# Last tile of a pooled-attention and SiLU kernel: where two VectorE sums stand, and which engine copies a PSUM bank

## The chip, the cores and the metric

The kernel runs on one core of a Trainium2 chip. The metric is device time in microseconds (us) of one execution, the median of several runs. The engines are called as the profile calls them: PE is TensorE (matmuls; PEld its weight loads), DVE is VectorE, ACT is ScalarE, POOL is GpSimd, SP is SyncE, which here only issues stores. The program orders each engine's instructions by hand, so that an instruction which waits holds up all that stand behind it on the same engine.

## What is computed

A pooled attention (8 batches, 8 heads, 576 tokens, head size 64; keys and values are means over 8 tokens) gives x with 4608 rows and 512 columns. A two-layer block follows:

```python
def _moe_ref(x, w_in, w_out):       # x 4608x512, w_in 512x2048, w_out 2048x512
    h = x @ w_in
    g = h * (1.0 / (1.0 + np.exp(-h)))
    return (g @ w_out).astype(np.float32)
```

The change touches only the last tile's part of `g @ w_out`.

## The kernel before, in words

The 4608 rows are worked in nine tiles of 512 (`NT` = 9). For each tile the kernel computes the transposed hidden values `h_T` (2048 x 512, bf16, 16 blocks of 128 partitions) and then the output tile; attention for the next tile is mixed in between. From tile 3 on, `run(t)` (L777) plays a list of tokens, `PROGRAM` (L769), one after another. Each token emits a few instructions, and since every engine works its own instructions in the order in which they are emitted, the token list is the order of every engine. `A`, `B`, `C`, `E` tokens make hidden values, `h1h` to `h7l` make sums of hidden values, `d10` to `d73` are quarters of products of the second matmul, `u1` and `u2` correct a partial sum.

The second matmul is split in quarters and done with seven products of sums in place of eight (`H_SUMS` L600, `W_SUMS` L618). Product n has its weights in `W_OUT[n]` and its left side in `h_sum[n]`, or straight from `h_T` for products 3 and 4. A product is 16 matmuls of 128x128 by 256 columns. Three PSUM banks collect them (`bank`, L698): P takes products 4, 2, 7, Q takes 3, 5, 6, and R takes 1. What each product is followed by is in `after` (L715):

- after 4, ScalarE copies P to `r_sb` (L718); after 3, VectorE writes `rr_sb` = Q + `r_sb` (L720)
- after 2, bank P holds M4 + M2, which is the lower left quarter of the output: ScalarE copies it to `o_sb[1]` (L722)
- after 5, bank Q holds M3 + M5, the upper right quarter: VectorE copies it to `o_sb[0]` (L726)
- `u1` and `u2` (L747 to L751) take these two quarters off `rr_sb`, which leaves -M2 - M5; GpSimd does this in tiles 3 to 7 and VectorE in the last
- after 1, VectorE writes `t_sb` = R + `rr_sb` (L730); after 7 and 6, P + `t_sb` (L732) and Q + `t_sb` (L736) are the other two quarters, and are stored

`hidden_sum` (L608) writes half of one `h_sum`, 128x1024 in bf16, and reads only `h_T`. Products 1, 2, 5, 6 and 7 need their two halves each.

The last tile (t = 8) has no attention beside it and no tile behind it. There `run` replaces everything from token `d10` on. The products 1, 7 and 6 are done by `columns` (L762) for half of each bank at a time, first columns 0 (`L0`), then columns 1 (`L1`), so that the first half can be summed and stored during the second. Before them come the sums that were still to do:

```python
            i = toks.index("d10")
            sums = [x for x in toks[i:] if x[0] in "hu"]
            toks = toks[:i] + sorted(sums) + ["L0", "L1"]
```

What is left of the list for the last tile, from the second half of the h sums on, is therefore

```
h5l h1h h1l h7h d20 d21 d22 d23 d50 d51 d52 d53 h6h h6l u1 u2 L0 L1
```

On VectorE this reads: four h sums, the copy of bank Q (L726, behind `d53`), the two halves of `h_sum6`, `u1`, `u2`, and then in `L0` the sums L730, L732, L736. On TensorE: products 2, 5, then 1, 7, 6 for columns 0, then 1, 7, 6 for columns 1. Product 6 needs `h_sum6` and writes bank Q; the columns 1 of product 1 write bank R, of which L730 reads columns 0. The stores of the last tile are issued by `store` (L551, the DMA at L555): the lower left quarter by GpSimd, the upper right by SP, in `L0` by SP and GpSimd, in `L1` by ScalarE and SP.

Of the kernel before, what the change touches and what calls it, by code (L numbers as in the profile page):

```python
# [36 lines left out]
def kernel(  # L37
# [9 lines left out]
    nc = tc.nc  # L47
# [43 lines left out]
    def ps_tile(shape, dtype, tag, name):  # L91
        return psum.tile(shape, dtype, tag=tag, bufs=banks[tag], name=name)
# [16 lines left out]
    o_sb = [singles.tile([128, 2, d_model], FP32, name=f"o_sb{n}") for n in range(2)]  # L109
# [26 lines left out]
    def load_q(b, halves=False):  # L136
        st = batches.setdefault(b, {})
        q_bf = mid.tile([128, 2, QI * D], BF16, tag="q_bf", name="q_bf")
        if halves:
            pass  # L140
        elif b == B - 1:

            for s in range(4):
                for a in range(2):
                    nc.gpsimd.dma_start(
                        out=q_bf[QP * s : QP * (s + 1), a, :].rearrange(
                            "p (i d) -> p i d", d=D
                        ),
                        in_=q[b, 4 * a + s].rearrange("(i p) d -> p i d", p=QP),
                    )  # L150
        else:
            nc.gpsimd.dma_start(out=q_bf, in_=q_r[b])
        st["q_bf"] = q_bf
        st["qT"] = mid.tile([128, 2, QI, QP, 2], BF16, tag="qT", bufs=1, name="qT")
# [41 lines left out]
    def behind_x_sums(n=6):  # L196
        nc.gpsimd.tensor_copy(out=gate[:1], in_=x_sum[:1, U_XI[n], 0, :1])
# [353 lines left out]
    def store(t, m, cs, engines=(nc.sync,)):  # L551
        n0 = (t * NTT + m * 128) // QP
        src = o_sb[m // 2][:, m % 2, cs]
        if n0 // QI == B - 1:
            engines[0].dma_start(out=out[n0 * QP : n0 * QP + 128, cs], in_=src)  # L555
            return
        for u in range(128 // QP):
            n = n0 + u
            rows = (
                out[n * QP : (n + 1) * QP] if n // QI == B - 1  # L560
                else out_r[n // QI, n % QI]
            )
            engines[u % len(engines)].dma_start(
                out=rows[:, cs], in_=src[QP * u : QP * (u + 1)]
            )
# [27 lines left out]
    LO, HI, FULL = slice(0, CQ), slice(CQ, 2 * CQ), slice(0, 2 * CQ)  # L593
# [37 lines left out]
    def left(n, kt, c):  # L631
        cs = slice(128 * c, 128 * (c + 1))
        if n in h_sum:
            return h_sum[n][:, kt, cs]
        i = n - 3
        return h_T[:, i * KQ + kt, i * NQ + 128 * c : i * NQ + 128 * (c + 1)]
# [59 lines left out]
    def down_stages(t, last):  # L696
        ps = {}
        bank = {2: "P", 5: "Q", 1: "R", 4: "P", 3: "Q", 7: "P", 6: "Q"}  # L698
        begun = set()
        r_sb, rr_sb, t_sb = r_sbs[0], rr_sbs[0], t_sbs[0]  # L700
        add, sub = ALU.add, ALU.subtract
        tt = nc.vector.tensor_tensor

        def matmuls(n, k0, k1, cs=(0, 1)):
            b = bank[n]
            for kt in range(k0, k1):
                for c in cs:
                    nc.tensor.matmul(  # L708
                        ps[b][:, c, :], lhsT=left(n, kt, c), rhs=W_OUT[n][:, kt, :],
                        start=b not in begun,  # L710
                        stop=kt == k1 - 1, skip_group_check=True,
                    )
                    begun.add(b)

        def after(n, cc=(0, 1), tail=False):  # L715
            cs = slice(cc[0], cc[-1] + 1)
            if n == 4:
                nc.scalar.copy(r_sb, ps["P"])  # L718
            elif n == 3:
                tt(out=rr_sb, in0=ps["Q"], in1=r_sb, op=add)  # L720
            elif n == 2:
                nc.scalar.copy(o_sb[1][:, :, LO], ps["P"])  # L722
                if last:
                    store(t, 3, LO, (nc.gpsimd,))
            elif n == 5:
                nc.vector.tensor_copy(out=o_sb[0][:, :, HI], in_=ps["Q"])  # L726
                if last:
                    store(t, 1, HI)
            elif n == 1:
                tt(out=t_sb[:, cs], in0=ps["R"][:, cs], in1=rr_sb[:, cs], op=add)  # L730
            elif n == 7:
                tt(out=o_sb[0][:, cs, LO], in0=ps["P"][:, cs], in1=t_sb[:, cs], op=add)  # L732
                for c in cc:
                    store(t, c, LO if tail else FULL, (nc.scalar if tail else nc.sync,))
            else:
                tt(out=o_sb[1][:, cs, HI], in0=ps["Q"][:, cs], in1=t_sb[:, cs], op=add)  # L736
                for c in cc:
                    if tail:
                        store(t, 3, HI, both)
                    else:  # L740
                        store(t, 2 + c, FULL, (nc.gpsimd if last else nc.sync,))

        def part_of(tok):
            if tok == "o":
                return after(6)
            n = int(tok[1])
            if tok[0] == "u":  # L747
                src = o_sb[1][:, :, LO] if n == 1 else o_sb[0][:, :, HI]
                (nc.vector if last else nc.gpsimd).tensor_tensor(  # L749
                    out=rr_sb, in0=rr_sb, in1=src, op=sub  # L750
                )  # L751
                return
            if not ps:
                for b in "PQR":
                    ps[b] = ps_tile([128, 2, CQ], FP32, "mm", f"o_ps{b}")
            i = int(tok[2])
            k0 = 2 * i if n == 4 else 2 * (i ^ 2)
            matmuls(n, k0, k0 + 2)
            if i == 3 and n != 6:
                after(n)  # L760

        def columns(c):  # L762
            for n in (1, 7, 6):
                matmuls(n, 0, KQ, (c,))
                after(n, (c,), c == 1)

        return part_of, columns
# [9 lines left out]
    def run(t):  # L777
        a = t + 1
        attn, last = a < B, t == NT - 1
        stage = unit_stages(t, iter(int, 1))  # L780
        part_of, columns = down_stages(t, last)
        toks = PROGRAM.split()
        gate_on = int([x for x in toks if x[0] == "x"][-1][1])
        attn_toks = ("T1 T2 k npp q0 q1 q2 q3 sc0 sc1 sc2 de0 de1 de2 nu0 nu1").split()
        if last:
            i = toks.index("d10")
            sums = [x for x in toks[i:] if x[0] in "hu"]
            toks = toks[:i] + sorted(sums) + ["L0", "L1"]
        toks = [x for x in toks if attn or x not in attn_toks]
        if a == B - 1:  # L790
            toks.insert(1 + max(toks.index("de2"), toks.index("nu1"), toks.index("o")), "nu2")
        if t == T4:
            toks.insert(0, "T2")
        if attn:
            if a + 1 < B - 1:
                load_q(a + 1)
            behind_x_sums(6 if t == T4 else gate_on)
            pool_k(a)
            if a + 1 < B:
                load_one(a + 1, "k")  # L800
            pool_v(a)
            if a + 1 < B:
                load_one(a + 1, "v")
                if a + 1 == B - 1:
                    load_q(a + 1)
                load_rest(a + 1, "k")
                load_rest(a + 1, "v")
        for x in toks:
            if x[0] in "ABCE" and x[1] in "2514376as":
                stage("ABCE".index(x[0]), {"a": "h"}.get(x[1], x[1]))  # L810
            elif x[0] == "L":
                columns(int(x[1]))
            elif x[:2] == "de":
                denominators(a, visits[int(x[2])])
            elif x[0] in "dou":
                part_of(x)
            elif x[0] == "h":
                k0 = 4 if x[2] == "h" else 0
                hidden_sum(int(x[1]), k0, k0 + 4)
            elif x == "T1":  # L820
                attn_tables()
            elif x == "T2":
                moe_tables()
            elif x == "k":
                k_transpose(a)
            elif x == "npp":
                numerators(a - 1, visits[2])
            elif x[0] == "q":
                n = int(x[1])
                q_transpose(a, n % 2, n // 2)  # L830
            elif x[:2] == "sc":
                scores(a, visits[int(x[2])])
            elif x[:2] == "nu":
                numerators(a, visits[int(x[2])])
            elif not last:
                unit_x_sum(t + 1, int(x[1]))
# [266 lines left out]
```

The softmax here doesn't subtract the row's maximum and nothing guards it: scores larger than these inputs give would overflow.

## Time and profile before

| | |
|---|---|
| time, median of 3 runs | 279.35 us (279.13 to 279.6) |
| span of the profiled execution | 277.0 us |
| PE busy | 270.7 us, 98% of the span |
| DVE busy | 241.2 us, 87% |
| ACT busy | 191.3 us, 69% |
| POOL busy | 114.3 us, 41% |
| an h sum in the last tile (L611) | 681 to 686 ns, ten of them |
| copy of bank P by ACT (L722) | 586 ns |
| copy of bank Q by DVE (L726) | 692 ns |
| last DVE instruction starts at | 273.96 us |

The page's busy shares are averages over all tiles. The chain of the profile follows the work that ended last back from the end, at each step to what released it; in the last tile it shows which engine sets the end at which moment. The timeline lists instructions by start, and merges neighbours that are alike (x4). In brackets stands how long the engine had been idle before one, and what released it. The token list's times are not in the program: they follow from the waits.

### The profile page before, as it was taken

The numbers are of one execution on the slowest core, as the hardware profiler recorded it, in microseconds if no ns is written. First come the engines' busy times: TensorE is split into PE (matmuls) and PEld (weight loads), VectorE is DVE, ScalarE is ACT, GpSimd is POOL, SyncE is SP. The second block draws the span as 40 slices with busy tenths as digits, with TensorE's granted clock in tenths as the row PEclk, the third lists the DMA queues.
The fourth block names the chain that finished last, engine by engine and source line by source line (L and its number), as shares of the span: only waits on it lengthen the run. The fifth ranks groups of instructions, "written<-read, shape, count | busy, mean of one in ns | idle before, by whom it ended". The sixth has DMA issues, their size and how long they took to land.

```text
span 277.0 us, 7372 instructions
## 1 busy us (share of the span) xinstructions
PE 270.7 (98%) x2923; PEld 209.1 (75%) x2933; DVE 241.2 (87%) x451; ACT 191.3 (69%) x373; POOL 114.3 (41%) x114
## 2 busy tenths in 40 slices
PE   8999999999999999999999999999999999999994
PEld 4448444576878678887888788877887788888883
DVE  4986787788998879998999899989999889998994
ACT  1688767468578966888778977798688858407700
POOL 8745217152158430954395428973720300040000
PEclk9999999999999999999999999999999999999999
DMA  7999999896849789669757835699510042014013
GB/s 210 285 254 247 206 321 183 239 160 123 165 56 210 212 123 176 151 169 134 129 113 196 126 56 127 178 109 146 132 43 0 2 105 50 2 27 128 1 38 116
DMA packets 31314, 37.73 MB, mean 136 GB/s; under 512 B 10352, under 2 KB 22256, under 8 KB 31280
## 3 DMA queue, kind: packets, MB, share of 16 engines
q0 software_dynamic: 23920, 27.03, 53.0%
q1 hardware_dynamic: 6928, 9.58, 12.6%
q10 hardware_dynamic: 432, 0.66, 0.7%
q8 instruction: 23, 0.38, 0.6%
q14 instruction: 11, 0.09, 0.1%
HBM read 36.70 MB, written 9.44 MB: 167 GB/s over the span
## 4 chain that ended last, share of the span: by engine, by line
PE 82%; DMA 12%; POOL 2%; DVE 1%; issue 1%; DVEq 0%; POOLq 0%
PE u_psP L489 14%; PE u_psQ L489 14%; PE o_psP L708 11%; PE o_psQ L708 11%; DMA w_in_sb<-in_moe_w_in_dram 7%; DMA w_out_sb<-in_moe_w_out_dram 6%; PE u_psR L489 5%; PE o_psQ L652 4%; PE o_psP L652 4%; PE o_psR L708 4%; PE hp_ps L543 4%; PE sc_ps L341 3%; PE nu_ps L385 3%; PE o_ps L578 2%; PE den_ps L359 2%; PE o_psR L652 1%
## 5 line engine op out<-in xcount | busy, mean ns | idle before, releaser
L489 PEld LDWEIGHTS <-w_sum 128*128 128x128 bf16 x532 | 51.9, 98 | 7.2 <-issue 0.3
L611 DVE TENSOR_TENSOR h_sum<-h_T 128x1024 bf16<-128x1024 bf16 (+1 forms) x78 | 55.7, 765 | 1.8 <-ACT h_T L549 1.0
L708 PEld LDWEIGHTS <-h_sum 128*128 128x128 bf16 x480 | 45.6, 98 | 9.5 <-issue 3.3
L349 ACT ACTIVATE es<-sc_ps 72x384 bf16<-72x384 f32 (+1 forms) x100 | 39.1, 471 | 6.2 <-PE sc_ps L341 6.0
L497 ACT ACTIVATE h_T<-c_sb 128x512 bf16<-128x512 f32 x58 | 35.6, 627 | 8.8 <-DVE c_sb L522 8.7
L749 POOL TENSOR_TENSOR rr_sb<-rr_sb,o_sb 128x512 f32<-128x512 f32 x10 | 16.9, 1687 | 42.3 <-ACT o_sb L722 36.5
L507 ACT COPY r_sb<-u_psP 128x512 f32<-128x512 f32 x29 | 17.0, 585 | 18.1 <-PE u_psP L489 17.9
L543 PE MATMUL hp_ps<-xT,w_in_sb 128*128 128x512 bf16 (+2 forms) x151 | 25.9, 317 | 0.3
L394 DVE TENSOR_TENSOR xT<-nu_ps,rec 128x384 bf16<-128x384 f32 (+1 forms) x50 | 23.9, 529 | 1.6 <-PE nu_ps L385 1.6
L489 PEld LDWEIGHTS <-w_in_sb 128*128 128x128 bf16 x232 | 22.5, 98 | 2.9
L191 POOL TENSOR_TENSOR raw<-raw 72x1024 f32<-72x1024 f32 x10 | 23.6, 2360 | 0.3 <-DMA raw<-in_v_dram 0.3
L522 DVE TENSOR_TENSOR c_sb<-u_psP,t_sb 128x512 f32<-128x512 f32 x29 | 19.8, 684 | 3.3 <-ACT r_sb L507 1.8
L549 ACT ACTIVATE h_T<-hp_ps 128x512 bf16<-128x512 f32 (+2 forms) x39 | 18.1, 476 | 5.9 <-PE hp_ps L543 4.8
L525 DVE TENSOR_TENSOR c_sb<-u_psQ,t_sb 128x512 f32<-128x512 f32 x29 | 19.9, 688 | 2.2 <-PE u_psQ L489 2.0
L510 DVE TENSOR_TENSOR rr_sb<-u_psQ,r_sb 128x512 f32<-128x512 f32 x29 | 19.8, 684 | 2.2 <-ACT r_sb L507 1.6
L513 DVE TENSOR_TENSOR t_sb<-u_psR,rr_sb 128x512 f32<-128x512 f32 x29 | 19.7, 681 | 1.6 <-PE u_psR L489 0.5
L543 PEld LDWEIGHTS <-w_in_sb 128*128 128x128 bf16 x156 | 14.6, 98 | 8.5 <-issue 0.7
L708 PEld LDWEIGHTS <-h_T 128*128 128x128 bf16 x192 | 18.8, 98 | 2.2
L497 ACT ACTIVATE h_T<-u_psQ 128x512 bf16<-128x512 f32 x29 | 17.2, 593 | 4.1 <-PE u_psQ L489 3.4
L497 ACT ACTIVATE h_T<-u_psP 128x512 bf16<-128x512 f32 x29 | 17.4, 599 | 2.7 <-PE u_psP L489 2.6
L368 ACT ACTIVATE lnd<-den_ps 128x384 f32<-128x384 f32 (+1 forms) x23 | 11.2, 487 | 11.3 <-PE den_ps L359 11.3
L489 PE MATMUL u_psP<-x_sum,w_in_sb 128*128 128x256 bf16 x116 | 17.6, 273 | 0.0
(105 smaller groups left out, 564.3 us busy)
## 6 DMA issues: line engine op xcount, KB each, us to landing
out_dram<-o_sb SPq DMA_DIRECT2D x128, 64.0 KB, 2.3
raw<-in_k_dram POOLq DMA_DIRECT2D x10, 576.0 KB, 8.2
raw<-in_v_dram POOLq DMA_DIRECT2D x10, 576.0 KB, 8.2
q_bf<-in_q_dram POOLq DMA_DIRECT2D x6, 576.0 KB, 11.1
w_in_sb<-in_moe_w_in_dram POOLq DMA_DIRECT2D x8, 256.0 KB, 8.6
w_out_sb<-in_moe_w_out_dram POOLq DMA_DIRECT2D x4, 512.0 KB, 13.3
raw<-in_v_dram POOLq DMA_DIRECT2D x2, 768.0 KB, 10.9
raw<-in_k_dram POOLq DMA_DIRECT2D x1, 768.0 KB, 10.9
```

The costliest lines, as they stand in the source:

```text
L191: nc.gpsimd.tensor_add(out=raw[:, :, : 2 * D], in0=raw[:, :, : 2 * D], in1=raw[:, :, 2 * D :])
L349: nc.scalar.activation(es[:, s, :], sc[s], func=AF.Exp, scale=score_scale)
L394: nc.vector.tensor_mul(out=xT[:, 2 * g0 + c : 2 * (g0 + ng - 1) + c + 1 : 2, cols], in0=nu[c][:, :w].rearrange("r (g n) -> r g n", g=ng), ...
L489: nc.tensor.matmul(ps[y, bank][:, u, :], lhsT=w[:, kk, 128 * u : 128 * (u + 1)], rhs=x[:, kk, :], start=first and u == 0 and kk == 0, stop ...
L497: nc.scalar.activation(h_T[:, g : g + 2, j * NQ : (j + 1) * NQ], src, func=AF.Silu)
L510: tt(out=rr_sb, in0=ps[y, "Q"], in1=r_sb, op=ALU.add)
L522: tt(out=c_sb[0], in0=ps[y, "P"], in1=t_sb, op=ALU.add)
L525: tt(out=c_sb[1], in0=ps[y, "Q"], in1=t_sb, op=ALU.add)
L543: nc.tensor.matmul(hp_ps[:, r0:r1], lhsT=w_in_sb[:, kk, g * 128 : (g + 1) * 128], rhs=xT[:, kk, x0 : x0 + r1 - r0], start=(kk == 0), stop= ...
L611: nc.vector.tensor_tensor(out=h_sum[n][:, ks, :], in0=quarter(*a, ks), in1=quarter(*b, ks), op=op)
L652: nc.tensor.matmul(ps[b][:, c, :], lhsT=left(n, kt, c), rhs=W_OUT[n][:, kt, :], start=b not in begun, stop=kt == k1 - 1, skip_group_check= ...
L708: nc.tensor.matmul(ps[b][:, c, :], lhsT=left(n, kt, c), rhs=W_OUT[n][:, kt, :], start=b not in begun, stop=kt == k1 - 1, skip_group_check= ...
```

## The change

In the last tile the two sums for `h_sum6` go ahead of token `d20`, so that on VectorE they follow the other four without anything between; they no longer stand behind the copy of bank Q. That copy goes to ScalarE, which already copies bank P. `u1` and `u2` stay right ahead of `L0`. Tiles 0 to 7 are as before. The purpose is to have VectorE work on the sums while products 2 and 5 still run, and to take the bank copy out of its row.

```diff
             elif n == 5:
-                nc.vector.tensor_copy(out=o_sb[0][:, :, HI], in_=ps["Q"])
+                copy = nc.scalar.copy if last else nc.vector.tensor_copy
+                copy(out=o_sb[0][:, :, HI], in_=ps["Q"])
                 if last:
                     store(t, 1, HI)
...
         if last:
-            i = toks.index("d10")
-            sums = [x for x in toks[i:] if x[0] in "hu"]
-            toks = toks[:i] + sorted(sums) + ["L0", "L1"]
+            i, j = toks.index("d10"), toks.index("d20")
+            sums = sorted(x for x in toks[j:] if x[0] == "h")
+            toks = toks[:j] + sums + [x for x in toks[j:i] if x[0] != "h"]
+            toks += ["u1", "u2", "L0", "L1"]
```

The last tile's list then ends in

```
h5l h1h h1l h7h h6h h6l d20 d21 d22 d23 d50 d51 d52 d53 u1 u2 L0 L1
```

## The prediction

> **What bounds the kernel now.** I read the page first: one core, span 277.0 us, TensorE (PE) busy 98% of it and granted full clock in all 40 slices. An average of 98% says that stages before the last tile are TensorE's; it says nothing of the last ten microseconds, and the diff touches nothing before them. So I went to the waits, the chain and the timeline of the last 15 us. First the waits between 262 and 278 us, longest first (who waited, for whom, us in total, times, longest):
>
> ```profile
> POOL out_dram L555 <- DVE o_sb L736: 5.1, 1, 5.1
> ACT o_sb L722 <- PE o_psP L708: 2.9, 1, 2.9
> PE o_psR L708 <- DVE t_sb L730: 0.8, 1, 0.8
> PEld L708 <- DVE h_sum L611: 0.5, 1, 0.5
> DVE o_sb L726 <- PE o_psQ L708: 0.3, 1, 0.3
> PE o_psQ L708 <- DVE h_sum L611: 0.2, 1, 0.2
> ```
>
> TensorE waits for VectorE (DVE) twice here: 0.2 to 0.5 us for h_sum and 0.8 us for t_sb. VectorE waits 0.3 us for TensorE ahead of its bank copy, L726. ScalarE (ACT) sits idle 2.9 us before L722.
>
> Then the chain of work that ended last, in order of time (start, length, what):
>
> ```profile
> 266.00 1.32 PE o_psQ L708 x12
> ...
> 267.95 1.28 DVE h_sum L611 x2
> 269.23 0.61 DVE rr_sb L749
> ...
> 269.87 0.70 DVE rr_sb L749
> ...
> 270.67 0.44 DVE t_sb L730
> ...
> 271.15 1.03 PE o_psR L708 x8
> 272.18 0.87 PE o_psP L708 x8
> 273.05 0.89 PE o_psQ L708 x8
> ...
> 273.96 0.42 DVE o_sb L736
> ```
>
> From 267.3 to 271.1 us the end is set by VectorE alone: the copy of bank Q, two h sums, u1 and u2 (both L749), the first t_sb. Before and after this stretch it is TensorE. The timeline of VectorE shows how its queue stands (start, length, line, operation, output and inputs):
>
> ```profile
> 264.53 2.49 DVE L611 TENSOR_TENSOR h_sum<-h_T 128x1024 bf16<-128x1024 bf16 x4
> 267.34 0.69 DVE L726 COPY o_sb<-o_psQ 128x512 f32<-128x512 f32 x1 [0.33 <-PE o_psQ L708]
> 267.95 1.28 DVE L611 TENSOR_TENSOR h_sum<-h_T 128x1024 bf16<-128x1024 bf16 x2
> 269.15 1.41 DVE L749 TENSOR_TENSOR rr_sb<-rr_sb,o_sb 128x512 f32<-128x512 f32 x2
> 270.67 0.42 DVE L730 TENSOR_TENSOR t_sb<-o_psR,rr_sb 128x256 f32<-128x256 f32 x1
> ```
>
> The reader is to see that VectorE has nothing to do from 267.02 (264.53 + 2.49) to 267.34, while the pair of sums queued behind the copy needs only h_T, whose last part ScalarE wrote by 262.26.
>
> **What the Trainium skill says.** "PSUM — Partial Sum Buffer", section "PSUM bank collisions raise a hardware error": two engines may not touch one bank in the same partitions at once, even in different columns, so the guard is by bank. That is why columns 1 of product 1 wait for the t_sb sum of columns 0, which reads the other half of bank R; the trace agrees (the 0.8 us wait; PE restarts at 271.15, 0.06 after t_sb ends). "Perfetto Trace Analysis", "Identifying Dependency Chains": an instruction that waits on several engines may get a separate semaphore instruction ahead of it. The trace agrees: t_sb, which needs DVE's u2 and PE's bank R, has one of 21 ns at 270.60, and starts 0.10 after u2 ends (270.67 against 270.57 in the chain), while u2, which needs DVE alone, starts 0.02 after u1. "ScalarE: Activation LUTs", "Table sets": copy is in every table set, so a second ScalarE copy loads nothing. L722 already copies among Silu with no load in this stretch. "SBUF — State Buffer", "Who interferes with whom": a VectorE sum with both inputs in SBUF contends with a GpSimd instruction that reads SBUF. The trace agrees, a tile earlier: the same pair of h sums took 2.42 us from 243.50, with GpSimd's L749 running to 245.37, against 1.28 us here. I come back to it.
>
> **The change, part by part.**
>
> (a) Two h sums move ahead of the bank copy. From 264.53 four sums take 2.49, one lasts 0.684 (L611, ten of them), so starts are (2.49 - 0.684)/3 = 0.60 apart. The pair then starts at 264.53 + 4 x 0.60 = 266.94 and not at 267.95, and ends at 266.94 + 1.28 = 268.22 and not at 269.23. That is 1.01 us, of two pieces: the idle 0.33 (0.40 if counted from the start that an unbroken row would have had) and the copy's 0.61 from start to start. Nothing ahead in the queue is delayed: all eight earlier sums keep their places, and the tokens move in VectorE's order alone.
>
> (b) Bank Q's copy goes from VectorE to ScalarE. It cost 0.692 there and should cost 0.586 here, by the row of L722, same shape and source (bank P). ScalarE has nothing after 266.23 but a store issue at 273.55. Q's last matmul ends at 267.30; with the 0.08 that L722 took behind bank P (265.56 to 265.64) the copy runs 267.38 to 267.97. Who waits for it: u2, the store of that half, and the first columns of product 6, which write bank Q. u2 cannot start before 268.86 (below); product 6's columns follow 8 + 8 matmuls at 0.87 a block, so not before 267.14 + 2 x 0.87 = 268.88. Both are some 0.9 us later than the copy's end. The store starts at the same time within 0.1. Cost on the path: nothing, hidden behind the sums and products 1 and 7.
>
> (c) What the copy's move adds as a wait: u2 now needs ScalarE (the copy) and VectorE (u1). Behind u2 stands t_sb, and for that TensorE waits, so any cost here is on the path. Bounds: 0, if ScalarE's part, met since 268.0, is taken early in the queue (u1 has such a semaphore instruction at 267.4, hidden), or 0.08, if u2 gets what t_sb has: a start 0.10 after its predecessor and not 0.02. I take 0.08, since in both VectorE's is the wait that is met last.
>
> (d) New times: u1 at 266.94 + (269.15 - 267.95) = 268.14; u2 at 268.14 + 0.72 + 0.08 = 268.94; t_sb 0.80 behind it at 269.74, ending 270.16. Before, it ended at 271.09: 0.93 earlier.
>
> (e) TensorE: product 1's columns 0 from 267.14, product 7's from 268.01, both as now. Product 6's wait for h_sum goes: sums done at 268.22, columns wanted at 268.88, and not 269.29. This 0.4 us alone is worth nothing, because TensorE then waits longer for t_sb: done with the block at 269.75, it could restart at 270.16 + 0.06 = 270.22. So 0.47 of waiting is left in place of 0.81, and VectorE still sets the end. This also bounds the gain: had VectorE taken no time, TensorE would restart at 269.75, 1.40 earlier than now.
>
> (f) From the restart on nothing changes: products 1, 7, 6 for columns 1, the last sum, its store. They shift whole. Last columns end at 273.94 - 0.93, last sum at 274.38 - 0.93 = 273.45. VectorE's two column-0 sums and GpSimd's store of half a tile are tied to t_sb and shift with it. Behind the last sum come 2.62 us to the span's end (277.0 - 274.38): a store issue of 0.33, landing about 1.7, closing semaphores. The two half-stores that don't shift were issued by 268.1 with about 2 us to land, so they are gone by then.
>
> Sum: -1.01 + 0.08 = -0.93 us. 279.35 - 0.93 = 278.42; I say 278.4.
>
> **Rivals.**
>
> The other wait takes its place. The end could be held by something between 267.3 and 271 that the chain hides: ScalarE's copy becoming visible late, or product 6 held for it. For that, the copy must end after 268.9, nearly 1 us later than L722's timing gives. If it held half of the gain back, 0.45 would be left: 278.9. Against it: the 0.9 us of slack on each of its readers. Chance 0.08.
>
> The stores set the end. DMA runs at 0.96 and 1.02 of its engines in two half-microseconds (272.5 to 273 and 273.5 to 274). If it were stores that end the kernel, an earlier last sum would only lengthen the wait, and the time would stay at 279.35. Against it: the last store has the normal landing of 1.7 us, and engines fall nearly idle in between (0.20 at 274 to 274.5). All big stores shift with the sums. Chance 0.06.
>
> The moved pair meets GpSimd, and the result is slower. GpSimd issues a store from 266.52 to 267.18, and the moved pair starts within that. If they contend as a tile earlier, the pair takes 2.42: it ends at 269.36, u1 starts 269.28, u2 270.08, t_sb 270.88, 0.21 later than now. That gives 279.35 + 0.21 = 279.56; with GpSimd's issue held up as well, 280. Against it: the two h sums that run during this issue today show no lengthening (all ten between 0.681 and 0.686). A store issue is not the fp32 sum of a tile earlier. Chance 0.04.
>
> **How the numbers follow.** Forecast 0.82; the three rivals 0.08, 0.06 and 0.04. Within the forecast the gain is 0.93 to 1.01 by (c), plus or minus 0.1 for semaphores whose place I can't see, and the runs before lie 0.25 around their median. So 279.35 - 1.1 - 0.25 = 278.0 below. Above, 279.35 - 0.8 + 0.2 = 278.75, extended to 278.95 to take in the half gain. What lies outside is the rivals of 0.06 and 0.04 and some scatter, under 2 in 10. 0.2% is 0.56 us, so faster means under 278.79: the forecast with a little scatter off, and a part of the first rival, 0.85. Same: 0.12. Slower, which needs over 279.91, takes a part of the last rival: 0.03.
>
> **What would show it.** In the profile after: six h sums in one row from 264.5, no copy on VectorE behind them; a second ScalarE copy near 267.4 of about 0.59; u1 near 268.1; t_sb near 269.7; no wait of TensorE for h_sum; its wait for t_sb about 0.4 to 0.5 and not 0.8; last sum near 273.4; some 2.6 us behind it. I am wrong if the sums lengthen while GpSimd issues its store, if u2 starts clearly after 268.95 (ScalarE's copy or its wait), or if more than 2.7 us stand behind the last sum.

## The result, and the profile after

The changed kernel takes 278.53 us (median of 6 runs, 278.02 to 278.85), against 279.35 before. The ratio of the times is 0.9967, with a 95% interval of 0.9954 to 0.998: 0.6 to 1.3 us faster, 0.9 in the middle. Beside the last experiments it was timed again: 278.47 (278.22 to 278.91, 11 runs) against 279.19, ratio 0.9975 (0.9966 to 0.9983), 0.5 to 0.9 us faster.

The page alone does not show this: the two spans read 277.0 and 276.9 us. The timeline of ScalarE tells why. Before, its first copy (a cast of the attention's pooled keys, `kz`) and a copy some 60 us later:

```profile
7.58 0.28 ACT L293 CAST kz<-kz_ps 128x144 bf16<-128x144 f32 x1 [4.55 <-PE kz_ps L286]
68.40 0.59 ACT L665 COPY r_sb<-o_psP 128x512 f32<-128x512 f32 x1
```

The same two in the changed kernel:

```profile
8.17 0.28 ACT L293 CAST kz<-kz_ps 128x144 bf16<-128x144 f32 x1 [5.20 <-PE kz_ps L286]
69.19 0.59 ACT L665 COPY r_sb<-o_psP 128x512 f32<-128x512 f32 x1
```

This execution was 0.59 us late at its first ScalarE copy and 0.79 late at 68 us, in a part that the diff does not touch, and it stays so. Product 5 on bank Q, before and after:

```profile
265.39 1.91 PE L708 MATMUL o_psQ<-w_out_sb,h_sum 128*128 128x256 bf16 x16
...
266.18 1.91 PE L708 MATMUL o_psQ<-w_out_sb,h_sum 128*128 128x256 bf16 x16
```

It ends at 265.39 + 1.91 = 267.30 before and at 266.18 + 1.91 = 268.09 after, in both 198.90 us behind the start of the copy at 68 us. So the last tile has to be compared from a mark of its own. I take this end of product 5 on bank Q, which the change does not move, and call it Qend.

VectorE's row in the last tile after the change (timeline: start, length, line, operation):

```profile
265.31 3.69 DVE L611 TENSOR_TENSOR h_sum<-h_T 128x1024 bf16<-128x1024 bf16 x6
268.91 1.48 DVE L750 TENSOR_TENSOR rr_sb<-rr_sb,o_sb 128x512 f32<-128x512 f32 x2
270.50 0.42 DVE L731 TENSOR_TENSOR t_sb<-o_psR,rr_sb 128x256 f32<-128x256 f32 x1
...
273.80 0.42 DVE L737 TENSOR_TENSOR o_sb<-o_psQ,t_sb 128x256 f32<-128x256 f32 x1 [0.45 <-PE o_psQ L708]
```

Six sums stand in one row where four, a gap, a copy and two stood. The pair u1, u2 takes 1.48 and not 1.41. ScalarE's row has the second copy:

```profile
268.17 0.59 ACT L727 COPY o_sb<-o_psQ 128x512 f32<-128x512 f32 x1 [1.16 <-PE o_psQ L708]
```

TensorE's one wait for VectorE in the last 15 us:

```profile
PE o_psR L708 <- DVE t_sb L731: 0.3, 1, 0.3
```

TensorE's wait for h_sum is gone, and its wait for t_sb is 0.3 and no longer 0.8. The chain (start, length, what) has u2's new semaphore instruction (`DVEq`) and still runs through VectorE before TensorE's restart:

```profile
259.90 0.34 PE u_psR L489 x3
...
262.38 2.28 DVE h_sum L611 x4
...
264.70 0.69 DVE rr_sb L720
...
265.91 3.09 DVE h_sum L611 x5
269.00 0.61 DVE rr_sb L750
269.61 0.03 issue
269.64 0.02 DVEq L750
269.66 0.04 issue
269.71 0.70 DVE rr_sb L750
...
270.50 0.44 DVE t_sb L731
...
270.98 1.03 PE o_psR L708 x8
```

It reaches further back than before. There VectorE's part began at Qend, because the copy in its row waited for product 5. Now it follows VectorE without a stop at TensorE back to 260.24, for more than 10 us; what VectorE still needs of product 5, u2's input by way of ScalarE's copy, is there in time. Qend is still a good mark, but no longer a cause.

Counted from Qend, the first t_sb sum starts at 2.41 and not 3.37, and the last sum ends at 6.13 (274.22 - 268.09) and not 7.08 (274.38 - 267.30): 0.95 us saved. Behind the last sum stand 2.68 us, before 2.62.

### The profile page after: what moved, and what is told of

Its sections match the earlier page's. It is cut to its first block, busy times and chain, and to the rows that moved or that the text cites. A ratio compares the mean times of both kernels' runs of the same rounds, so it can differ in the third digit from the quotient of the medians.

```text
span 276.9 us, 7384 instructions
## 1 busy us (share of the span) xinstructions
PE 271.9 (98%) x2933; PEld 210.0 (76%) x2933; DVE 240.7 (87%) x450; ACT 192.1 (69%) x374; POOL 114.6 (41%) x114
## 4 chain that ended last, share of the span: by engine, by line
PE 79%; DMA 15%; DVE 4%; issue 1%; POOL 0%; DVEq 0%; POOLq 0%
PE u_psP L489 14%; PE u_psQ L489 14%; PE o_psP L708 10%; PE o_psQ L708 10%; DMA w_in_sb<-in_moe_w_in_dram 6%; DMA w_out_sb<-in_moe_w_out_dram 6%; PE u_psR L489 5%; PE o_psQ L652 4%; PE o_psP L652 4%; PE hp_ps L543 4%; PE o_psR L708 4%; PE sc_ps L341 3%; PE nu_ps L385 3%; PE o_ps L578 2%; DMA q_bf<-in_q_dram 2%; DVE h_sum L611 2%
## 5 line engine op out<-in xcount | busy, mean ns | idle before, releaser
L543 PE MATMUL hp_ps<-xT,w_in_sb 128*128 128x512 bf16 (+2 forms) x156 | 26.6, 319 | 0.0
```

The lines of the kernel that those rows point to most:

```text
L543: nc.tensor.matmul(hp_ps[:, r0:r1], lhsT=w_in_sb[:, kk, g * 128 : (g + 1) * 128], rhs=xT[:, kk, x0 : x0 + r1 - r0], start=(kk == 0), stop= ...
```

## The experiments

All of them in one table, by their own traces; times are medians, in us. They were timed in three sets, each beside its own runs of the kernel before, whose medians were 279.37, 279.38 and 279.19; the ratios are against these. Times of different sets can be compared by their ratios only.

| kernel | first t_sb behind Qend | last sum behind Qend | behind the last sum | time | ratio to before (95%) |
|---|---|---|---|---|---|
| before | 3.37 | 7.08 | 2.62 | 279.35 | |
| changed | 2.41 | 6.13 | 2.68 | 278.53 | 0.9954 to 0.998 |
| sums ahead only | 2.94 | 6.66 | 2.68 | 278.86 | 0.9975 to 0.9991 |
| copy on ScalarE only | 2.42 | 6.13 | 2.60 | 278.26 | 0.995 to 0.9975 |
| u2 ahead of u1 | 2.35 | 6.07 | 2.69 | 278.11 | 0.9939 to 0.9964 |
| one more ScalarE copy | 2.42 | 6.14 | 2.64 | 278.4 | 0.9957 to 0.9975 |
| three more ScalarE copies | 3.17 | 6.88 | 2.63 | 279.13 | 0.9985 to 1.0003 |
| no u1, u2 | 0.92 | 5.70 | 2.67 | 277.77 | 0.9932 to 0.9962 |
| u1 on GpSimd | 2.69 | 6.41 | 2.63 | 278.49 | 0.9966 to 0.9984 |
| u1, u2 by columns | 1.82 | 5.80 | 2.59 | 277.99 | 0.9938 to 0.9965 |
| the same, again | 1.82 | 5.78 | 2.70 | 278.0 | 0.9945 to 0.9972 |
| by columns, L733 first | 1.82 | 5.70 | 2.70 | 278.18 | 0.9954 to 0.9979 |
| changed, again | 2.42 | 6.14 | 2.62 | 278.47 | 0.9966 to 0.9983 |

The interval from Qend agrees to 0.02 between the two executions of each kernel that was traced twice, while the times of one kernel scatter by up to 0.7 us to a side, once by 1.7 (u1 on GpSimd, 280.18 the longest of 20): the trace decides where the times can't. What stands behind the last sum is known to 0.1 us only, since the span is given to a tenth.

### One half of the change alone: the sums ahead, the copy left on VectorE

Against the changed kernel:

```diff
-                copy = nc.scalar.copy if last else nc.vector.tensor_copy
+                copy = nc.vector.tensor_copy
```

> The two h sums stand ahead of product 2, but bank Q's copy stays on VectorE. Times are counted from the end of product 5 on bank Q (Qend); with the kernel before the first t_sb sum starts at 3.37 and the last sum ends at 7.08 behind it, with the changed kernel at 2.41 and 6.13. My theory: the change is worth two separate pieces of VectorE's row, the idle time ahead of the copy (0.33 to 0.40) and the copy itself (0.61); this kernel gets the first only: t_sb at 2.97 to 3.04, last sum near 6.7, time near 279.0. Rival: the sums' early place is what counts (my part (a) put both pieces down to it): t_sb at 2.4, last sum 6.1, 278.5.

VectorE's row in this kernel:

```profile
264.48 3.69 DVE L611 TENSOR_TENSOR h_sum<-h_T 128x1024 bf16<-128x1024 bf16 x6
268.09 0.69 DVE L727 COPY o_sb<-o_psQ 128x512 f32<-128x512 f32 x1
268.69 1.41 DVE L750 TENSOR_TENSOR rr_sb<-rr_sb,o_sb 128x512 f32<-128x512 f32 x2
```

The gap is filled, but the copy stands in the row, 0.60 from its start to u1's. The last sum ends at 6.66, 0.42 earlier than before, and t_sb starts at 2.94, a little ahead of the 2.97 to 3.04 expected. That is my theory's first piece and no more. u1 and u2 take 1.41 again, as both of u2's inputs now come from VectorE.

### The other half alone: the copy on ScalarE, the sums left behind product 5

Against the kernel before:

```diff
-                nc.vector.tensor_copy(out=o_sb[0][:, :, HI], in_=ps["Q"])
+                copy = nc.scalar.copy if last else nc.vector.tensor_copy
+                copy(out=o_sb[0][:, :, HI], in_=ps["Q"])
```

> Only bank Q's copy goes to ScalarE; the two h sums stay behind product 5 in the list. My theory: with the copy gone nothing of VectorE's stands between the fourth and the fifth h sum in either list, so its row is that of the changed kernel: six sums unbroken, t_sb at 2.41 behind Qend, last sum at 6.13, time 278.5. Rival: the sums' place in the list counts by itself; then the pair would start only after product 5 and t_sb near 2.8 to 3.0, time near 279.0.

```profile
265.09 3.69 DVE L611 TENSOR_TENSOR h_sum<-h_T 128x1024 bf16<-128x1024 bf16 x6
268.70 1.48 DVE L750 TENSOR_TENSOR rr_sb<-rr_sb,o_sb 128x512 f32<-128x512 f32 x2
```

This is the changed kernel's row: six sums unbroken, last sum at 6.13, 278.26 us. The list still names `h6h` and `h6l` after `d53`, but nothing of VectorE's is left between, so the order of VectorE's instructions is the same as in the changed kernel. The rival, that the place in the list counts by itself, falls. The half of the diff that moves the sums is worth 0.42 us alone and nothing once the copy has left VectorE. This is read from the traces; the times of this kernel and of the changed one come from different sets.

### u2 ahead of u1

```diff
-            toks += ["u1", "u2", "L0", "L1"]
+            toks += ["u2", "u1", "L0", "L1"]
```

> The changed kernel with u2 ahead of u1. u2 then waits for ScalarE alone, and u1 for VectorE alone, so neither of them has a wait on two engines. Theory: the 0.08 us that I put down to u2's second wait goes away: u1 starts 0.02 to 0.03 behind u2's end and not 0.10, t_sb at 2.33 behind Qend, last sum at 6.05; the time moves by less than can be measured, 278.45. Rival: the 0.08 is no matter of the number of waits, and t_sb stays at 2.41.

The chain of this kernel at the same place:

```profile
268.36 0.61 DVE rr_sb L750
268.97 0.02 issue
269.00 0.70 DVE rr_sb L750
```

The semaphore instruction between the two is gone, and the second starts 0.03 after the first and not 0.10. t_sb starts at 2.35, 0.06 earlier than in the changed kernel. The Trainium skill's "Perfetto Trace Analysis", "Identifying Dependency Chains", says that such an instruction may stand ahead of one that waits on several engines; here it costs 0.06 to 0.08 us on the path. I put that down to VectorE's own wait being met last: in the kernel with three more copies, below, ScalarE's is met last, and u2 starts 0.03 behind the copy's end (270.16 - 270.13). The time, 278.11, can't confirm so small a thing by itself.

### One and three more copies on ScalarE

```diff
+                for _ in range(1 if last else 0):
+                    nc.scalar.copy(r_sb, ps["Q"])
                 copy(out=o_sb[0][:, :, HI], in_=ps["Q"])
```

The second kernel has 3 in place of 1.

> The changed kernel with one more ScalarE copy of bank Q (to r_sb, which nobody reads any more) ahead of the real one. Theory: the real copy ends 0.67 behind Qend in the changed kernel and is wanted at 1.58 (product 6) and 1.62 (u2), so 0.9 us is to spare. One more copy moves its end to about 1.2: t_sb stays at 2.41, last sum at 6.13, 278.5. Rival: ScalarE's copy is on the path; then both move by 0.5.

With one more, the real copy starts 0.48 after the added one, ends at 1.11 behind Qend, and nothing else moves: last sum at 6.14.

> The changed kernel with three more ScalarE copies of bank Q ahead of the real one. Theory: its end moves to about 2.3 to 2.5 behind Qend, 0.7 to 0.9 past what is to spare; u2 starts at 2.4 to 2.6, TensorE waits for product 6 too, t_sb starts near 3.2 to 3.4, last sum near 6.9 to 7.1, time 279.3: the whole gain is lost. Rival: the spare time is larger than I worked out, and the loss stays under 0.4.

With three more, the real copy and u2 in the timeline:

```profile
269.54 0.59 ACT L729 COPY o_sb<-o_psQ 128x512 f32<-128x512 f32 x1
...
270.16 0.69 DVE L752 TENSOR_TENSOR rr_sb<-rr_sb,o_sb 128x512 f32<-128x512 f32 x1 [0.86 <-ACT o_sb L729]
270.18 1.03 PE L708 MATMUL o_psQ<-w_sum,h_sum 128*128 128x256 bf16 x8 [0.65 <-ACT o_sb L729]
```

Now ScalarE's copy is waited for by both of its readers. It ends at 270.13 - 267.79 = 2.34, which is 1.67 later than in the changed kernel, and 0.75 of it reach the last sum (6.88). So 0.92 us were to spare, as worked out. t_sb starts at 3.17, just ahead of the 3.2 to 3.4 expected. The time, 279.13, has lost most of the gain; with a ratio of 0.9985 to 1.0003 it can't be told from the kernel before.

### Without u1 and u2

```diff
-            toks += ["u1", "u2", "L0", "L1"]
+            toks += ["L0", "L1"]
```

> The changed kernel without u1 and u2, so two quarters of the last tile are left uncorrected. Theory: VectorE's row then ends with the h sums, 0.8 behind Qend; t_sb starts when bank R is there, near 1.0; TensorE runs products 1, 7, 6 and again 1, 7, 6 with no wait and restarts at about 2.45 and not 2.89. Last sum near 5.7, time near 278.1: that is all that is left for any further work on this stretch of VectorE. Rival: the stores set the end; then more than 2.7 us stand behind the last sum and the time stays at 278.5.

This kernel leaves out the correction of two quarters and so shows what is left when VectorE's row is shorter. The chain then is TensorE alone, from Qend until the last sum's bank is done:

```profile
267.63 0.87 PE o_psR L708 x8
268.51 0.87 PE o_psP L708 x8
269.38 0.87 PE o_psQ L708 x8
270.25 0.87 PE o_psR L708 x8
271.13 0.87 PE o_psP L708 x8
272.00 0.89 PE o_psQ L708 x8
...
272.91 0.42 DVE o_sb L737
```

TensorE restarts columns 1 at 270.09 - 267.63 = 2.46 (its timeline start), against 2.89 in the changed kernel. The last sum ends at 5.70, and 2.67 us stand behind it, much as everywhere else. The stores' rival falls: they follow the last sum, whenever it comes. And 0.43 us was all that VectorE still held back in the changed kernel.

### u1 on GpSimd

```diff
                 nc.scalar.copy(o_sb[1][:, :, LO], ps["P"])
                 if last:
+                    nc.gpsimd.tensor_tensor(
+                        out=rr_sb, in0=rr_sb, in1=o_sb[1][:, :, LO], op=sub
+                    )
                     store(t, 3, LO, (nc.gpsimd,))
...
-            toks += ["u1", "u2", "L0", "L1"]
+            toks += ["u2", "L0", "L1"]
```

> The changed kernel with u1 on GpSimd, right behind ScalarE's copy of bank P and ahead of GpSimd's store; it then runs beside the last four h sums, as GpSimd's u1 does in the tiles before. This tests the mechanism of my third rival. If such a sum on GpSimd contends with the h sums, as the 2.42 us pair of the tile before suggests, the six sums take some 4.8 us and not 3.69, and t_sb starts near 2.8 behind Qend, last sum near 6.5, 278.9. If it does not contend, the six sums take 3.69 and t_sb starts near 1.7, last sum near 5.7, 278.1.

The lines of the h sums and of GpSimd, the first with minimum, median and maximum of one in ns:

```profile
L611 DVE TENSOR_TENSOR h_sum<-h_T x6: 677/684/1759, 265.0 to 269.1; 128x1024 bf16<-128x1024 bf16 x6
```

```profile
264.98 4.76 DVE L611 TENSOR_TENSOR h_sum<-h_T 128x1024 bf16<-128x1024 bf16 x6
266.76 1.84 POOL L724 TENSOR_TENSOR rr_sb<-rr_sb,o_sb 128x512 f32<-128x512 f32 x1 [20.94 <-ACT o_sb L722]
```

One of the six took 1.759 us and the row 4.76: they do contend, as the Trainium skill's "SBUF — State Buffer", "Who interferes with whom", says of a VectorE sum with both inputs in SBUF and a GpSimd instruction that reads SBUF. u1's 0.80 us (from its start to u2's) leave VectorE's row and 1.07 come in, so t_sb starts at 2.69, a tenth ahead of the 2.8 expected, and the last sum ends 0.28 later than in the changed kernel. The times differ by no more than they scatter (278.49). The last section shows that it is GpSimd's sum, and not its store, that does this.

### u1 and u2 by columns

Columns 0 of both stand ahead of the first t_sb sum, columns 1 behind it. The new function also works u2's part (from `o_sb[0]`) ahead of u1's, which the experiment "u2 ahead of u1" showed to be worth 0.06 us by itself:

```diff
+        def correct(c):
+            for src in (o_sb[0][:, c, HI], o_sb[1][:, c, LO]):
+                nc.vector.tensor_tensor(
+                    out=rr_sb[:, c, :], in0=rr_sb[:, c, :], in1=src, op=sub
+                )
+
         def columns(c):
             for n in (1, 7, 6):
+                if n == 1 and c == 0:
+                    correct(0)
                 matmuls(n, 0, KQ, (c,))
                 after(n, (c,), c == 1)
+                if n == 1 and c == 0:
+                    correct(1)
...
-            toks += ["u1", "u2", "L0", "L1"]
+            toks += ["L0", "L1"]
```

> The changed kernel with u1 and u2 cut by columns: columns 0 of both (each 256 wide, about 0.42 us) stand ahead of the first t_sb sum, columns 1 behind it. Theory: VectorE still sets TensorE's restart in the changed kernel, by the 0.27 us wait that its trace shows, and TensorE alone would restart at 2.45 behind Qend and not at 2.89. With t_sb starting near 1.75 and ending near 2.2 TensorE becomes the bound: no wait for t_sb, last sum near 5.7, time near 278.1. Rival: columns 1 come too late for the second t_sb sum, or product 7 waits longer for bank P, as four sums now stand ahead of L733: then 0.3 of it is lost again, last sum near 6.0, 278.4.

> The version with u1 and u2 by columns (columns 1 ahead of L733) once more, beside the changed kernel. Theory: last sum at 5.80, 0.33 ahead of the changed kernel, time 278.0 to 278.1. If its lead was luck: equal to the changed kernel, 278.4.

The chain of the first of the two:

```profile
269.93 0.87 PE o_psR L708 x8
270.81 0.96 PE o_psP L708 x8
```

TensorE waits for t_sb no more. The last sum ends at 5.80 and, in the second trace, 5.78. One of the blocks takes 0.96 and not 0.87: product 7's columns 1 go on at 270.73 and L733, which reads bank P, ended at 270.26 + 0.42 = 270.68. So a small part of the rival is true. With 277.99 (277.73 to 278.19) and 278.0 us (277.74 to 278.05) this version had the lowest median in both sets of runs. The changed kernel, timed beside the second, took 278.22 to 278.91, above all of its five times. Against the kernel with only u2 ahead of u1 (last sum at 6.07), cutting by columns itself brings 0.27 to 0.29 us of the 0.33 to 0.36.

The last version has `n == 7` in place of the second `n == 1`, so that L733 comes first:

> u1 and u2 by columns as before, but columns 1 of both stand behind the first sum on bank P (L733) and not ahead of it. In the version with them ahead, TensorE took 0.96 for the block on bank R and not 0.87, since product 7's columns 1 had to wait for L733 (ended 0.05 before TensorE went on), and the last sum ended at 5.80 behind the end of product 5 on bank Q, against 5.70 without any u1 and u2. Theory: the 0.1 comes back, L733 ends 0.6 earlier, last sum at 5.70 to 5.72, time 277.9. Rival: the second t_sb sum or L737 now come so late that TensorE waits for bank Q; then 5.8 or more.

```profile
270.32 0.87 PE o_psR L708 x8
271.20 0.87 PE o_psP L708 x8
```

The 0.09 comes back, and the last sum at 5.70 is where it was without any u1 and u2. The time, 278.18 (277.94 to 278.45), does not show it: this difference is smaller than the scatter, and which of the two versions is the faster stays open by time.

> The changed kernel once more, beside the two versions by columns on the same chip. Theory: last sum at 6.13 behind the end of product 5, time 278.3 to 278.5. If the versions by columns were only lucky with the start of the kernel, this one comes out as fast as they do, 278.0.

The changed kernel's second trace gave 2.42 and 6.14, so the lead of the versions by columns is no luck of the start.

## Why the prediction was right, point by point

**Place of the bound.** Right: VectorE's row ahead of t_sb set the end. Each kernel that shortened or lengthened it moved the last sum, until TensorE alone was left at 5.70 (without u1 and u2, and by columns), and 2.59 to 2.70 us stood behind the last sum in all of them.

**(a), size right, cause put wrong.** The step said 1.01 us for "two h sums move ahead of the bank copy", as a filled gap of 0.40 and the copy's 0.61, and put both under the sums' move. The sizes hold: 0.42 for the gap (sums ahead only), and another 0.53 when the copy leaves, which is 0.61 less 0.08 for u2's wait. But the whole is got by moving the copy, without moving a sum. The sums were held up by the copy alone; when it goes, they come forward of themselves. The number came out because both halves were in the diff; for the sums alone the step would have been off by the copy's 0.61. I should have written down VectorE's order for each half of the diff, and would have seen that once the copy is gone, moving the sums leaves it unchanged.

**(b).** Right to the hundredth: the copy ran from 0.08 to 0.67 behind Qend, and the added copies measured 0.92 us to spare, where I had said some 0.9.

**(c).** Right within 0.02: the 0.08 was taken from the wait that t_sb already had. u2 starts 0.10 behind u1's end and not 0.02 to 0.03, and t_sb comes 0.06 earlier when the order is turned.

**(d), (e).** t_sb came 0.96 earlier by Qend against 0.93 forecast. TensorE's wait for h_sum went. What it then waited for t_sb I put at 0.47; measured against the kernel with no u1 and u2 it is 0.43. But I set this 0.47 beside the wait view's 0.81, and they are counted differently. The view counts from the end of a block of 8 matmuls, which it shows 1.04 long, though the next block starts 0.87 behind it: 270.98 - (269.67 + 1.04) = 0.27. Counted by starts the wait is 270.98 - (269.67 + 0.87) = 0.44 after and 271.15 - (269.29 + 0.87) = 0.99 before. So the sign that I named, a wait of 0.4 to 0.5 in the view, did not come (0.27), though the restart did.

**(f).** Right: the rest shifted whole, and what stands behind the last sum was 2.68 in place of 2.62.

**Sum.** Forecast -0.93, in the trace -0.95, in the times -0.82 and, timed again, -0.72. The forecast 278.4 lies among the runs.

**Rivals.** The late copy is refuted by the two kernels with more copies, the stores by the kernel without u1 and u2. The third rival's mechanism is real but its trigger was not: a GpSimd sum stretches h sums, GpSimd's store issue does not. In the changed kernel the issue (267.31, 0.66 long) lies beside the fourth and fifth sums, and the six still took 3.69, starts 0.60 apart.

## What to carry to other kernels

Write out each engine's order for each half of a change, since a move in the program that crosses no instruction of that engine leaves its order as it is: here the moved sums brought nothing once the copy was gone (last sum at 6.13 with and without). When an instruction goes to another engine, count the wait that its reader gains on two engines (0.06 to 0.08 us here) and how long the new place may be late before anyone notices (0.92 us here). Where a wait is left, ask which part of the result the waiting engine needs first: cutting u1 and u2 by columns, with u2's part first, brought the last sum forward by a further 0.33 us without removing any work. VectorE even worked longer on them (two pieces of 0.88 us in place of 1.48), but half of that now lies behind t_sb.

## What the runs showed that I had not expected

The first quarter of the kernel differs between executions by about as much as the change brings. The first ScalarE copy began between 7.45 and 8.31 us in the thirteen traces, whose programs are the same up to the last tile, and the copy at 68 us between 68.36 and 69.19. From there to Qend all of them took 198.90 or 198.91 us. So whatever differs ahead of the last tile differs before 68 us. The first copy alone doesn't tell how late an execution will be: the kernel before and the one with only the copy moved began at 7.58 and 7.57, and stood at 68.40 and 68.97. In the second of them TensorE waited 0.4 us for the load of `w_out_sb` on the way, in the first there is no such wait. So the arrival of loads is a part of it there; how much in the others was not tried. (SP does not only issue stores here: it issues two of the early loads of keys.) It follows that spans of single profiles can't be compared here, and stretches from a common mark can.

Contention with GpSimd fell on one h sum. In the kernel with u1 on GpSimd, u1 ran from 266.76 to 268.60; the sum before it and the one that started with it kept some 0.68 us, the next took 1.759, to about 0.55 past u1's end:

```profile
267.39 2.36 DVE L611 TENSOR_TENSOR h_sum<-h_T 128x1024 bf16<-128x1024 bf16 x2
```

GpSimd's store issue follows u1 at 268.55, 0.66 long, so it lies beside the end of this sum too. The kernel before shows that the issue is not needed. In tile 7 GpSimd works u1 and u2 and issues no store:

```profile
241.85 3.52 POOL L749 TENSOR_TENSOR rr_sb<-rr_sb,o_sb 128x512 f32<-128x512 f32 x2 [23.44 <-ACT o_sb L722]
```

There too the h sum that started 0.03 after u1 kept 0.68. The one that started at 244.16, while GpSimd's u2 (243.77 to 245.37) was running, took 1.75 and ended 0.55 past u2's end. In tiles 3 to 6 the pair of h sums beside u2 took 2.35 or 2.36 in place of 1.28. So it is GpSimd's sum that holds an h sum up. Why it falls on one instruction as a whole, and not on the one that starts with it, was not tried.
